# Attention with a mixture of experts: the sixth batch's late routing steps and scatters, and the fifth's last scatters, moved behind pair 28

## The chip, the cores and the metric

The kernel runs on one NeuronCore of a Trainium2 chip. Its engines work at the same time, each through its own instructions in program order: PE (TensorE, matrix products), DVE (VectorE), ACT (ScalarE), POOL (GpSimd) and SP (SyncE, which here only issues transfers). The metric is the device time of one execution in microseconds.

## The reference, cut to what matters

```python
B, H, S, D = 8, 8, 576, 64
scores = (rotate(q) @ rotate(k).T) / sqrt(D)
attn = exp(scores - max(scores)); attn = attn / sum(attn)
x = transpose(attn @ v).reshape(B * S, H * D)          # 4608 tokens of 512
logits = x @ w_gate + modality_bias[modality_id]       # 8 experts
e_idx = argmax(logits); gate_w = softmax(logits)[e_idx]
for e in range(8):                                     # each token: its one expert
    out[e_idx == e] = gate_w * (relu(x @ w1[e]) @ w2[e])
```

## The kernel before, in words

**Attention.** The 64 heads go through as 32 pairs (`n` = 0 to 31), four to a batch. For a pair, POOL rotates q and k by four passes over tiles of 128x1152 (`rope_`, lines 461 to 469; ACT makes the high part of the result between the last two), SP copies the two halves of the result across the partitions (`swap`, line 477, tile SW), PE makes nine score tiles (`scores`, line 492), DVE copies each out of PSUM with its minimum (`rowmin`, line 501, tile `sc`), ACT takes the exponentials (`expo`, line 510), PE turns them over (`fill`, line 515; F0 to F3 are four such fills), ACT and DVE each copy one of the two banks of a fill (`evac`, lines 548 and 452), PE multiplies by v (`AV`, line 573) and makes the pair's output rows and gate logits (`outp`, line 608). PSUM is four tiles of two banks, `ps0` to `ps3`, which stand in the traces as ps and in the lists of order as ps_126 to ps_129; `take` gives a step the slot that the table SLOTS names if its banks are free, and another free one if not.

**Routing of a batch.** After its fourth pair (3, 7, ..., 31) a batch is routed in fifteen small steps, RK0 to RK14 (`route`): logits, one-hot choice (RK6, three POOL operations, tile OH), ranks within the expert (RK8, seven small matmuls on PE with a PSUM bank of their own), RK9 (DVE adds the running counts and so frees the bank), RK10 (ACT), RK11 (`own_rank`, POOL), RK12 (DVE, the gate values into VAL), RK13 (DVE, tile `of`), RK14 (POOL, row numbers `oi`). Then VO writes the token numbers and gates beside the batch's rows in the DRAM tensor X (`vout`, two small transfers, lines 640 and 641), and for each of five groups of tokens BK loads the group's rows from X into one of two buffers XL (`back`, lines 756 and 758, 257 KB, the fifth half that) and SC scatters them to the rows of their experts in the DRAM tensor XS (`scatter`, line 738, an indirect transfer that only POOL issues). The buffers are given out in turn, so a BK waits until the SC before the last has read its buffer.

**The expert stage.** A first plan (`plan0`, POOL and DVE, done at about 405 us) covers five supers of 512 or 256 rows out of the first five batches alone; it needs the fifth batch's scatters, not the sixth's. The rest is planned after the eighth batch. Super 0 runs inside the last pair, super 1 is `m_plain`, the next are `m_super`. A super's results leave PSUM through ACT into the `sc` buffers (`m_store`, line 1113) and go to the output by indirect transfers that POOL issues (line 1114). The pool has NSS = 4 `sc` buffers, so the sixth result tile (super 1, fourth tile) takes the buffer of the second (super 0, second tile).

**What sets the order.** Every step of attention and routing is a job with a key, `KEYS[name]` or the pair's own entry in EDGE, plus 14.438 (PER) times the pair's number; jobs are sorted by key and written out in that order on all engines. Keys behind those of the last pair's end (about 472.56) come after the PSUM of attention is given back. The batch's last pair gives its routing keys, so the fifth batch's are pair 19's and the sixth's pair 23's; at key 404.26 pair 28 begins. In the trace a key is roughly the microsecond at which its step runs.

Of the kernel before, what the change touches and what calls it, by code (L numbers as in the profile page):

```python
# [19 lines left out]
B, H, S, D = 8, 8, 576, 64  # L20
# [110 lines left out]
        "LD1": -42.214,  # L131
    },
    19: {
    },
    23: {
    },
    25: {
        "RE": 11.575, "F2": 13.246, "A_F2": 14.351, "B_F2": 14.486, "RI": 16.427, "AVB": 18.725, "OTB": 20.519, "OUT": 26.426,
# [92 lines left out]
def tile_attention_moe(ctx: ExitStack, tc: tile.TileContext, qk, v, mod, wg, mb, w1, w2, rope, cf, ci, out):  # L231
    nc = tc.nc
# [405 lines left out]
    def vout(b, eng=nc.sync):  # L638
        xd = X[b * S:(b + 1) * S, DM:XU]
        eng.dma_start(out=xd[0:512, :].rearrange("(p j) w -> p j w", j=4), in_=VAL[:, b, 0:4, :].bitcast(F32))  # L640
        eng.dma_start(out=xd[512:576, :], in_=VAL[0:64, b, 4, :].bitcast(F32))
# [93 lines left out]
    def scatter(b, j):  # L735
        oi = bt_[b]["oi"]
        n = P if j < 4 else 64
        inst = nc.gpsimd.indirect_dma_start(  # L738
            out=XS, out_offset=bass.IndirectOffsetOnAxis(ap=oi[0:n, j:j + 1], axis=0),
            in_=xl[b, j][0:n], in_offset=None, bounds_check=E * RS - 1, oob_is_err=False).ins  # L740

        for _b, x in placed:
            tc.declare_no_dep(inst, x, reason="rows of other tokens")
        placed.append((b, inst))
        if b >= NPL:
            for x in taken:
                tc.declare_no_dep(inst, x, reason="the first plan's blocks lie before the rows of later batches")
# [4 lines left out]
    def back(b, j, eng=nc.sync):  # L752
        t = xl[b, j] = XL[len(xl) % 2]
        xd = X[b * S:(b + 1) * S, 0:XU]
        if j < 4:
            eng.dma_start(out=t[:, 0:XU], in_=xd[0:512, :].rearrange("(p j) w -> j p w", j=4)[j])
        else:
            eng.dma_start(out=t[0:64, 0:XU], in_=xd[512:576, :])

    def pads():  # L760
        nc.vector.tensor_copy(CNT, RUN[0:1, B, :])
        for e in range(E):
            r = nc.sync.value_load(CNT[0:1, e:e + 1], min_val=0, max_val=E * RS - BLK)
            inst = nc.sync.dma_start(out=XS[bass.ds(r, BLK), 0:XU], in_=ZR[:, :]).ins
            for _b, x in placed:
                tc.declare_no_dep(inst, x, reason="rows behind those of the tokens")
            for x in taken:
                tc.declare_no_dep(inst, x, reason="the first plan's blocks are full")
            placed.append((B, inst))
# [692 lines left out]
    def J(k_, nm, n, f, *a):  # L1462
        jobs.append((k_ + PER * n, len(jobs), f, a))
# [30 lines left out]
    for n in range(NPAIR):  # L1494
        def K_(nm, f, *a):
            J(EDGE.get(n, {}).get(nm, KEYS[nm]), nm, n, f, *a)

        for u in range(9):
            K_(f"S{u}", scores, n, u)
            K_(f"MN{u}", rowmin, n, u)  # L1500
            K_(f"EX{u}", expo, n, u)
        for f in ("F0", "F1", "F2", "F3", "FA", "FB"):
            K_(f, fill, n, f)
            for g in range(2):
                K_(f"{'AB'[g]}_{f}", evac, n, f, g)
        for w in range(2):
            c = "AB"[w]
            K_(f"AV{c}", AV, n, w)
            K_(f"OT{c}", avout, n, w)
            K_(f"EV{c}", ev, n, 1 - w)  # L1510
        K_("OUT", outp, n)
        for w in range(2):
            K_("R" + "EI"[w], rsum, n, w)
        if n > 0:
            for part, nm in ((1, "T1"), (0, "T2"), (2, "R"), (3, "HI"), (4, "LO")):
                K_(nm, rope_, n, part)
            for i in range(2):
                K_("SW" + "HL"[i], swap, n, i)
        K_("LV", loadv, n)
        if n > 2:  # L1520
            K_("LD1", load, n, 1)
            K_("LD", load, n, 0)
        if n % 4 == 3:
            K_("BIAS", bias, n // 4)
            K_("XO", xout, n // 4)
            steps = [(f,) for f in route(n // 4)]
            scats = [(scatter, n // 4, j) for j in range(5)]
            if n == z:

                planned = plan()  # L1530
                steps[0:2] = [(each, lambda f: f(), *steps[0:2])]
                late = steps + [(lambda: [vout(B - 1, nc.gpsimd)] + [(back(B - 1, j, nc.gpsimd), scatter(B - 1, j)) for j in range(5)] + [pads()],)] + [(each, next) + ((planned, None),) * 4] * 13
                continue
            for i, x in enumerate(steps):
                K_(f"RK{i}", *x)
            eng = nc.sync if n // 4 < B - 2 else nc.gpsimd
            K_("VO", vout, n // 4, eng)
            for i, x in enumerate(scats):
                K_(f"BK{i}", back, n // 4, i, eng)
                K_(f"SC{i}", *x)  # L1540
# [209 lines left out]
```

## Time and profile before

| | us |
|---|---|
| median of three runs (lowest, highest) | 882.19 (881.38, 886.98) |
| the profiled execution, its own time | 884.29 |
| its span in the trace | 882.5 |

A row of the trace gives the start in microseconds from the span's start, the duration, the engine, the line of the kernel, the operation, its output and inputs, and in brackets how long the engine stood idle before it and what ended that. PE is the engine with the most work; a microsecond in which it stands idle is one that the kernel could lose.

### The profile page before, as it was taken

The page shows a single profiled execution, that of the slowest core. Times are in us where ns is not written, and L with a number is a line of the kernel's source. Part 1 is how long each engine was busy: PE and PEld are TensorE (multiplying, and loading weights), DVE is VectorE, ACT ScalarE, POOL GpSimd, SP SyncE. Part 2 cuts the span into 40 slices and gives each one's busy share as a digit, 9 for nine tenths or more (in the row PEclk, how much of TensorE's full clock was granted, in tenths as well). Part 3 has the DMA queues.
Part 4 walks back from the last instruction along what each step waited for, and adds up shares of the span by engine and source line. Part 5 has one row for each costly group of instructions (what it writes and reads, how often), then busy time and mean ns, then how long its engine had stood idle before and what let it go on. Part 6 is the DMA issues. An engine that isn't in the chain of part 4 may idle for free.

```text
span 882.5 us, 24889 instructions
## 1 busy us (share of the span) xinstructions
PE 833.9 (94%) x9528; PEld 688.7 (78%) x9528; DVE 708.9 (80%) x1595; ACT 612.2 (69%) x1311; POOL 453.5 (51%) x365
## 2 busy tenths in 40 slices
PE   2899999999999999888999999999999999999992
PEld 2677777777777777676778989898989898989882
DVE  6888898888898888777888577989898998979360
ACT  2898989889888888777975446464656474748360
POOL 2999979989899898999511211024201112020100
PEclk9999999999999999999999999999999999999996
DMA  8877868979788797875877961377955413530520
GB/s 262 229 231 193 260 169 259 265 211 283 205 262 245 215 279 205 249 213 171 251 213 187 328 181 49 60 219 224 282 139 186 114 38 88 169 101 8 186 73 14
DMA packets 116330, 165.80 MB, mean 188 GB/s; under 512 B 31180, under 2 KB 76894, under 8 KB 116204
## 3 DMA queue, kind: packets, MB, share of 16 engines
q1 hardware_dynamic: 107468, 139.18, 55.2%
q0 software_dynamic: 7392, 23.34, 7.5%
q8 instruction: 77, 1.26, 0.6%
q10 hardware_dynamic: 1344, 1.62, 0.6%
q14 instruction: 49, 0.40, 0.1%
HBM read 118.14 MB, written 34.70 MB: 173 GB/s over the span
## 4 chain that ended last, share of the span: by engine, by line
PE 79%; DMA 5%; POOL 4%; ACT 4%; DVE 3%; issue 2%; SPq 1%; ACTq 0%; POOLq 0%; DVEq 0%
PE psY L1326 20%; PE ps L573 15%; PE psH L1202 14%; PE ps L492 13%; PE ps L515 9%; PE ps L608 2%; DMA SW<-HL 2%; PE psY L1202 2%; ACT P L510 1%; PE psH L1084 1%; PE psY L1103 1%; DMA ST<-in_rope_dram 1%; POOL HL L469 1%; DVE sc L501 1%; DMA ST<-in_moe_w_dram 1%
## 5 line engine op out<-in xcount | busy, mean ns | idle before, releaser
L501 DVE CUSTOM_DVE_ANT_1 sc<-ps,ZERO 128x576 f32<-128x576 f32 x288 | 206.6, 748 | 24.0 <-PE ps L492 11.3
L510 ACT ACTIVATE P<-sc,mn 128x576 f32<-128x576 f32 x256 | 195.5, 767 | 5.9 <-DVE mn L501 4.7
L492 PE MATMUL ps<-HL 64*128 64x288 f32 x960 | 167.9, 309 | 13.7 <-ACT HL L452 10.8
L492 PE MATMUL ps<-SW 64*128 64x288 f32 x960 | 168.1, 309 | 7.6 <-DMA SW<-HL 7.5
L1114 POOL DMA_INDIRECT out_dram<-sc,ix x36 | 43.4, 1206 | 222.1 <-ACT sc L1113 215.4
L492 PEld LDWEIGHTS ps<-HL 64*128 64x128 f32 x960 | 134.4, 188 | 19.5 <-ACT HL L452 10.8
L492 PEld LDWEIGHTS ps<-SW 64*128 64x128 f32 x960 | 134.3, 188 | 11.9 <-issue 9.4
L573 PE MATMUL ps<-PH,AT 128*64 128x320 f32 (+1 forms) x1024 | 139.6, 415 | 4.0 <-DVE PH L548 3.7
L1202 PE MATMUL psH<-HL,W1H 128*128 128x256 f32 x600 | 126.4, 279 | 0.4 <-ACT HL L452 0.4
L1202 PE MATMUL psH<-HL,W1L 128*128 128x256 f32 x400 | 111.6, 279 | 0.0
L573 PEld LDWEIGHTS ps<-PH,AT 128*64 128x64 f32 x1024 | 68.4, 137 | 53.1 <-DVE PH L548 7.0
L548 DVE COPY PH<-ps 128x512 f32<-128x512 f32 (+1 forms) x160 | 98.3, 630 | 11.0 <-PE ps L515 8.8
L452 ACT ACTIVATE PH<-ps 128x512 f32<-128x512 f32 (+1 forms) x160 | 85.3, 551 | 29.6 <-PE ps L515 26.0
L515 PEld LDWEIGHTS ps<-idf,P 64*128 64x128 f32 x2304 | 86.0, 138 | 20.7 <-ACT P L510 8.5
L1326 PE MATMUL psY<-W2L,SW 128*128 128x512 f32 x256 | 101.3, 396 | 0.0
L1326 PE MATMUL psY<-W2H,SW 128*128 128x512 f32 x256 | 100.9, 394 | 0.0
L515 PE MATMUL ps<-idf,P 64*128 64x64 f32 x2304 | 97.3, 225 | 2.8 <-ACT AT L452 1.7
L1202 PEld LDWEIGHTS psH<-HL,W1H 128*128 128x128 f32 x600 | 98.8, 188 | 1.1 <-ACT HL L452 0.6
L469 POOL TENSOR_TENSOR HL<-ST,HL 128x1152 fp32r<-128x1152 f32 x31 | 82.5, 2660 | 24.4 <-ACT HL L452 24.3
L465 POOL TENSOR_TENSOR ST<-ST 128x1152 f32<-128x1152 f32 x30 | 79.5, 2651 | 1.1
L738 POOL DMA_INDIRECT XS<-XL,oi x40 | 44.8, 1120 | 66.1 <-DMA XL<-X 45.2
L1202 PEld LDWEIGHTS psH<-HL,W1L 128*128 128x128 f32 x400 | 75.2, 188 | 0.0
(286 smaller groups left out, 1829.6 us busy)
## 6 DMA issues: line engine op xcount, KB each, us to landing
ST<-in_moe_w_dram SPq DMA_DIRECT2D x88, 512.0 KB
ST<-in_qk_dram SPq DMA_DIRECT2D x62, 576.0 KB
SW<-HL SPq DMA_DIRECT2D x124, 216.0 KB
AT<-in_v_dram SPq DMA_DIRECT2D x32, 256.0 KB
X<-X SPq DMA_DIRECT2D x8, 1024.0 KB
XL<-X SPq DMA_DIRECT2D x24, 257.0 KB
XG<-XS SPq DMA_DIRECT2D x40, 128.0 KB
XS<-ZR SPq DMA_DIRECT2D x8, 514.0 KB
```

The source lines that it names most:

```text
L452: return nc.scalar.activation(o, i, AF.Copy, scale=scale)
L465: e.tensor_tensor(a, a, b, op=ALU.add)
L469: e.tensor_tensor(d["HL"][:, 1, o], a, d["HL"][:, 0, o].bitcast(F32), op=ALU.subtract)
L492: nc.tensor.matmul(ps[:, g, 0:288], t[:, wq, q0:q0 + P], t[:, wk, k0:k0 + 288], start=(m == 0), stop=(m == len(L) - 1))
L501: nc.vector.tensor_tensor_reduce(sc, d.pop(("S", u))[:, :, 0:288], ZERO.unsqueeze(2).to_broadcast([P, 2, 288]), 1.0, FMAX, ALU.add, ALU.mi ...
L510: nc.scalar.activation(p, sc.rearrange("p a b -> p (a b)"), AF.Exp, bias=mn, scale=-1.0, accum_out=d["sum"][:, u:u + 1])
L515: nc.tensor.transpose(ps[:, g, c:c + 64], src[r, k0:k0 + P], idf[r, r])
L548: alone(d["at", f], g, (nc.vector.tensor_copy if g else acopy)(o, i).ins, int(f[1] in "23B"))
L573: i = nc.tensor.matmul(pa[hh * 64:hh * 64 + 64, 0:c1 - c0], d["V"][:, hh, kt, :], r, start=(kt == 0), stop=(kt == 4))
L738: inst = nc.gpsimd.indirect_dma_start(out=XS, out_offset=bass.IndirectOffsetOnAxis(ap=oi[0:n, j:j + 1], axis=0), in_=xl[b, j][0:n], in_off ...
L1202: nc.tensor.matmul(ps[b][:, r * BLK:r * BLK + BLK], w[:, c, f0:f0 + P], x[:, c, :], start=(first and r == 0 and c == 0 and i == 0), stop=( ...
L1326: nc.tensor.matmul(po[t], hx[:, c, o:o + P], w[:, c, :], start=(k == 0 and c == 2 * q and i == 0), stop=(k == 3 and c == 2 * q + 1 and i = ...
```

## The change

The fifth batch (index 4, pair 19) keeps its steps, but its loads and scatters take another order, 0, 1, 3, 2, 4, and the last two scatters come 9 and 31 key units later. The sixth batch (index 5, pair 23) has RK6 to RK8 some three units earlier (RK9 two later), RK10 to RK14 22 to 64 units later, and VO, the loads and the scatters after them, in the order 3, 4, 2, 1, 0, at keys 461 to 470, just ahead of the seventh batch's. Its VO and its five BK are issued by POOL in place of SP.

```diff
     19: {
+        "BK0": 71.4, "BK1": 71.5, "BK3": 95.0, "BK2": 116.0, "BK4": 131.0,
+        "SC3": 113.825, "SC2": 128.215, "SC4": 152.075,
     },
     23: {
+        "VO": 129.3, "BK3": 130.0, "BK4": 130.1, "BK2": 132.5, "BK1": 133.0, "BK0": 137.0,
+        "RK6": 45.016, "RK7": 49.391, "RK8": 52.824, "RK9": 58.16, "RK10": 79.988, "RK11": 109.721, "RK12": 128.347, "RK13": 128.956,
+        "RK14": 129.684, "SC3": 130.859, "SC4": 132.359, "SC2": 132.942, "SC1": 136.961, "SC0": 137.506,
     },
...
-            eng = nc.sync if n // 4 < B - 2 else nc.gpsimd
+            eng = nc.sync if n // 4 < B - 3 else nc.gpsimd
             K_("VO", vout, n // 4, eng)
             for i, x in enumerate(scats):
                 K_(f"BK{i}", back, n // 4, i, eng)
```

The new lines move the line numbers behind them by five (line 701 is 706 in the lists of the change). Three places show what moves.

On PE, in pair 27, before: the six score matmuls into ps_126 and the fill of ps_129 (F3), then the sixth batch's ranks (tile OH) in ps_127:

```order
L492 MATMUL ps_126<-HL_87 128x288
L492 MATMUL ps_126<-SW_89 128x288
L492 MATMUL ps_126<-HL_87 128x288
L492 MATMUL ps_126<-SW_89 128x288
L492 MATMUL ps_126<-HL_87 128x288
L492 MATMUL ps_126<-SW_89 128x288
L515 MATMUL ps_129<-idf,P_120 128x64 x16
L701 LDWEIGHTS UT
L701 MATMUL ps_127<-OH,UT 128x48
L703 LDWEIGHTS ON
L703 MATMUL ps_127<-OH,ON 128x40
```

And now, the end of the ranks and what follows it:

```order
L708 LDWEIGHTS ON
L708 MATMUL ps_127<-OH,ON 128x16
L708 LDWEIGHTS ON
L708 MATMUL ps_127<-OH,ON 128x8
L497 MATMUL ps_126<-HL_87 128x288
L497 MATMUL ps_126<-SW_89 128x288
L497 MATMUL ps_126<-HL_87 128x288
L497 MATMUL ps_126<-SW_89 128x288
L497 MATMUL ps_126<-HL_87 128x288
L497 MATMUL ps_126<-SW_89 128x288
L520 MATMUL ps_129<-idf,P_120 128x64 x16
L613 MATMUL ps_128<-RW,AT 64x72 x18
```

The ranks moved ahead of six matmuls and a fill, and the pair's output matmuls (line 613, before 608) now follow the fill at once. At their new place bank 1 of ps_127, which DVE empties, is not free yet in the order of the jobs, so `take` gives them bank 0, which ACT empties.

On POOL, at the same time, before (tiles ST and HL are the rotation; `rk` is RK11, `pes` the first plan):

```order
L463 TENSOR_TENSOR ST_75<-ST_75 128x1152
L738 DMA XS<-XL_82,oi 39424x528
L687 TENSOR_TENSOR vv<-vv,vm 128x40
L688 TENSOR_SCALAR OH<-vv 128x32
L689 TENSOR_SCALAR OH<-vv 64x8
L469 TENSOR_TENSOR HL_86<-ST_74,HL_86 128x1152
L461 TENSOR_TENSOR ST_75<-ST_75,ST_74 128x1152
L465 TENSOR_TENSOR ST_75<-ST_75 128x1152
L738 DMA XS<-XL_83,oi 39424x528
L718 TENSOR_TENSOR rk<-rk,OH 128x40
L738 DMA XS<-XL_82,oi 39424x528
L831 TENSOR_SCALAR pes<-pes 1x1
```

And now:

```order
L692 TENSOR_TENSOR vv<-vv,vm 128x40
L693 TENSOR_SCALAR OH<-vv 128x32
L694 TENSOR_SCALAR OH<-vv 64x8
L468 TENSOR_TENSOR ST_75<-ST_75 128x1152
L474 TENSOR_TENSOR HL_86<-ST_74,HL_86 128x1152
L743 DMA XS<-XL_82,oi 39424x528
L466 TENSOR_TENSOR ST_75<-ST_75,ST_74 128x1152
L470 TENSOR_TENSOR ST_75<-ST_75 128x1152
L836 TENSOR_SCALAR pes<-pes 1x1
```

Two of the fifth batch's scatters and RK11 are gone from this stretch; the scatters come back behind the plan, and the one-hot choice is ahead of a rotation pass. From here to the last rotation pass POOL issues three scatters in place of five, and none in place of three between there and the sixth batch's new tail.

On POOL, behind the last rotation, the sixth batch's whole tail now stands ahead of the seventh's. It begins with:

```order
L645 DMA X<-VAL 512x1x2
L646 DMA X<-VAL 64x2
L723 TENSOR_TENSOR rk<-rk,OH 128x40
L733 CAST oi<-of 128x5
L761 DMA XL_83<-X 128x514
L763 DMA XL_82<-X 64x514
L743 DMA XS<-XL_83,oi 39424x528
L743 DMA XS<-XL_82,oi 39424x528
L761 DMA XL_83<-X 128x514
L743 DMA XS<-XL_83,oi 39424x528
L761 DMA XL_82<-X 128x514
L743 DMA XS<-XL_82,oi 39424x528
```

It goes on with the load and the scatter of group 0, the seventh batch's VO, its cast, two loads, super 0's first store to the output (line 1119, before 1114), the seventh batch's other loads and scatters, and then the second store. Before, the seventh batch's VO stood first in this row, and the stretch held its ten transfers only. On SP the sixth batch's two VO and five BK transfers are gone.

## Rows read from the trace of the kernel before

**Rows 1.** Page, part 1: busy us of each engine (share of span) xinstructions
```profile
PE 833.9 (94%) x9528; PEld 688.7 (78%) x9528; DVE 708.9 (80%) x1595; ACT 612.2 (69%) x1311; POOL 453.5 (51%) x365
```

**Rows 2.** Busy time in one stretch: engines' busy us, TensorE clock, DMA share, GB/s
```profile
380.00:450.00 70.00, 62.84 (x1004) 47.52 (x1002) 53.54 (x160) 55.93 (x146) 49.45 (x60) 1.00 0.71 208
```

**Rows 3.** Timeline of PE: start, us, engine line op out<-in [idle before <-releaser]
```profile
387.12 0.40 PE L492 MATMUL ps<-HL 64*128 64x288 f32 x1 [0.87 <-ACT AT L452]
...
389.36 0.20 PE L701 MATMUL ps<-OH,UT 128*128 128x48 bf16 x1 [1.08 <-DVE PH L548]
...
389.60 0.86 PE L608 MATMUL ps<-RW,AT 64*64 64x72 f32 x36
...
391.44 1.95 PE L573 MATMUL ps<-PH,AT 128*64 128x256 f32 x16 [0.34 <-DVE RUN L710]
...
416.53 1.64 PE L515 MATMUL ps<-idf,P 64*128 64x64 f32 x46 [1.68 <-ACT AT L452]
...
443.06 0.37 PE L492 MATMUL ps<-SW 64*128 64x288 f32 x1 [1.54 <-DMA SW<-HL]
```

**Rows 4.** Timeline of ACT, 374 to 446 us
```profile
385.96 0.85 ACT L452 ACTIVATE PH<-ps 128x512 f32<-128x512 f32 x2
...
414.99 1.16 ACT L452 ACTIVATE HL<-ST 128x1152 fp32r<-128x1152 f32 x1 [4.01 <-POOL ST L465]
```

**Rows 5.** Timeline of DVE, 374 to 500 us
```profile
397.66 0.18 DVE L721 RECIPROCAL VAL<-ee 128x5 f32<-128x5 f32 x1
397.76 0.14 DVE L783 TENSOR_REDUCE pes<-cmp 1x5 f32<-1x40 f32 x1
...
460.64 0.70 DVE L1063 STREAM_TRANSPOSE XG<-XG 128x512 f32<-128x512 f32 x1
```

**Rows 6.** Timeline of POOL, 385 to 480 us
```profile
397.99 0.18 POOL L831 TENSOR_SCALAR pes<-pes 1x1 f32<-1x1 f32 x1 [1.48 <-DVE pes L783]
...
410.71 0.18 POOL L728 CAST oi<-of 128x5 int32<-128x5 f32 x1
411.18 1.10 POOL L738 DMA_INDIRECT XS<-XL,oi  x1 [0.29 <-POOL oi L728]
412.31 2.64 POOL L465 TENSOR_TENSOR ST<-ST 128x1152 f32<-128x1152 f32 x1
```

**Rows 7.** Timeline of SP's queue, 380 to 505 us
```profile
435.14 0.54 SPq L756 DMA_DIRECT2D XL<-X  x1
435.77 4.55 SPq L477 DMA_DIRECT2D SW<-HL  x4
```

**Rows 8.** DMA issues by line: count, KB each, median us from issue to landing
```profile
XL<-X POOLq DMA_DIRECT2D x8, 257.0 KB, 5.5
...
XS<-XL,oi POOLq DMA_INDIRECT x40, 6.3
out_dram<-sc,ix POOLq DMA_INDIRECT x36, 4.6
```

**Rows 9.** Timeline of POOL, 465 to 640 us
```profile
481.09 1.15 POOL L756 DMA_DIRECT2D XL<-X  x2 [0.44 <-issue]
...
501.26 0.59 POOL L756 DMA_DIRECT2D XL<-X  x1 [6.54 <-DMA XS<-XL,oi]
...
513.78 0.98 POOL L1114 DMA_INDIRECT out_dram<-sc,ix  x1 [0.30 <-issue]
...
593.92 1.03 POOL L738 DMA_INDIRECT XS<-XL,oi  x1 [8.19 <-DMA XL<-X]
```

**Rows 10.** Timeline of ACT, 495 to 552 us
```profile
535.73 0.69 ACT L1113 ACTIVATE sc<-psY,ix 128x512 f32<-128x512 f32 x1 [0.70 <-issue]
537.13 0.60 ACT L452 ACTIVATE AT<-psH 128x512 f32<-128x512 f32 x1 [0.71 <-PE psH L1202]
538.53 0.60 ACT L452 ACTIVATE AT<-psH 128x512 f32<-128x512 f32 x1 [0.80 <-PE psH L1202]
...
541.26 1.06 ACT L452 ACTIVATE W1H<-ST 128x1024 fp32r<-128x1024 f32 x1 [0.67 <-ACT HL L452]
```

## The prediction

> **What bounds the kernel now.** I read the page's busy times first: PE works 94% of the span [rows 1], so a change of this kind can only move PE's idle time, or make more of it. Then the stretch that the change touches, by windows: from 380 to 450 us PE is busy 62.84 of 70 us and idle 7.2 [rows 2]. The timeline of PE shows where those go, and the reader is to see the releaser in the brackets [rows 3]: 0.87 us for an ACT copy, 1.08 ahead of the sixth batch's ranks, 0.34 for the step that frees the ranks' bank, 1.68 behind an ACT copy at 416.53, 1.54 for the swapped tile SW at 443.06; the other 1.7 us of the 7.2 are waits that no edited step releases. The 1.68 is really POOL's: ACT stood 4.01 us at 414.99 for the rotation pass of line 465, and the copy that PE wanted was queued behind it [rows 4]. So in this stretch PE is bound, with POOL's rotations and SP's swaps coming last now and then.
>
> **The ranks go ahead of a fill (gain 1.4 us).** Before, the ranks wanted the bank that DVE empties, and DVE came to it late: PE waited 1.08 us, and the matmuls behind the ranks, the pair's output and the product with v, could not pass [rows 3]. Now the ranks stand before the six score matmuls. Those had to wait 0.87 us anyway for ACT to empty ps_126, until 387.12 [rows 3]; the ranks' new bank is emptied by ACT in the copy at 385.96, the first of two in 0.85 us, so by about 386.5 [rows 4], and OH is earlier than before, as POOL makes it ahead of a 2.64 us pass. The ranks (some 0.25 us, 389.36 to 389.60) thus fit into the 0.87 us, and the 1.08 us has nothing left that it waits for: the output matmuls only want a tile whose minimum DVE took before. The 0.34 us goes too, since the product with v takes another slot than that of the ranks. Together 1.42. Bounds: 1.42 above; below nothing, if the output or the product is then held by DVE's copies, which keep their order and are what PE waited for.
>
> **POOL is lighter, but little of it counts (gain 0.5 us).** Ahead of the plan two scatters of about 1.1 us and RK11 are gone. That buys nothing: POOL already waited 1.48 us at 397.99 for DVE's `pes` [rows 6], so leaving earlier it waits longer. What counts is that `pes` itself comes earlier with PE (the 1.4 us of above) and without the VAL reciprocal ahead of it (0.18 us, of which 0.1 until the next starts [rows 5]). Behind the plan POOL runs without a gap to the pass at 412.31 that ACT waited for [rows 6]. In that piece one scatter (1.10) stays, a group of the fifth batch in place of one of the sixth, and the `oi` cast with the wait behind it goes (0.18 + 0.29 = 0.47). So this pass ends 1.4 + 0.1 + 0.5 = 2.0 us earlier, PE comes there 1.4 earlier, and of its 1.68 us wait 0.5 to 0.6 falls away. Bounds: 0 to 0.6.
>
> **SP is lighter (gain 0.6 us).** The 4.55 us of swaps for the last pair stood behind a BK of the sixth batch that took 0.63 us of SP, from 435.14 to 435.77 [rows 7]; PE then waited 1.54 for them at 443.06 [rows 3]. Without it they start 0.63 earlier. The five loads and VO leave SP's other swaps unhindered as well, but PE waited for none of those. Less traffic (the sixth batch's loads and scatters, four and a half groups of 257 KB [rows 8] each way, 2.3 MB, out of a stretch where DMA is busy 0.71 [rows 2]) may add something; bounds 0 and the whole 1.54.
>
> **DVE pays at the other end (loss 0.35 us).** RK12 and RK13, 0.18 us each by the VAL row [rows 5], move to the transpose of super 0's rows at 460.64, where DVE works without a gap until super 0's weights are split. Behind them stand the weight splits that PE's first expert matmuls want. I take the full 0.35; nothing at the least.
>
> **The tail on POOL (cost 0, up to 10 us).** The sixth batch's seven loads and writes and five scatters now stand ahead of the seventh's on POOL, and what is queued behind both is super 0's second store, at 513.78 before [rows 9]. Who waits for it: its `sc` buffer is the one that ACT needs for super 1's fourth tile, at 535.73, and ACT has 0.71 + 0.80 + 0.67 = 2.2 us of idle time from there until the copy at 541.26 [rows 10]. So the store may land until 535.7 + 2.2 = 537.9 without cost; beyond that ACT, PE's next, is late by the rest.
>
> When does it land? VAL now comes just ahead of the transposes at 460.64 [rows 5], so the tail starts at 461. Of it POOL must wait, in turn, for VO's landing, for one scatter (group 3, whose buffer the third load takes) and for four loads. The landings are 6.3 and 5.5 us at the median [rows 8]: 6.3 + 4 x 5.5 = 28.3; VO's I put at half a load's, 3; the issues between are two of 0.6 and four scatters of 1.1 [rows 6, 9], 5.6. That is 37 us, so the seventh batch's VO comes at 498, and its first loads, 4.2 later, at 502 in place of 481.09 [rows 9]: 21 us late. From those loads to the second store it was 513.78 - 481.09 = 32.7 us, which puts the store at 534.9 and its landing, 4.6 on [rows 8], at 539.5. In that stretch two scatters took 7.5 us each (6.54 of wait and 1.0 of issue [rows 9]); they now lie behind 515 us, when the transfers of the weights thin out, and at the median of 6.3 take 2.4 less: 537.1. That is 0.8 us inside the limit, so I take 0. Both ends: the seventh batch's loads can be absorbed further (nothing), or the sixth's four loads take 8.2 us each, as the one of the eighth batch did that POOL waited for at 593.92 [rows 9]: 10.8 later, landing at 548, cost 10. The gains of above move both times alike.
>
> For a transfer that POOL issues the Trainium skill (DMA: Bandwidth & Descriptors, section Anatomy of one DMA — SWDGE (gpsimd) path) gives about 2.0 us and the bytes at 436 GB/s, 2.6 us for 257 KB. The rows show twice that, 5.5 and 6.3, on a loaded chip [rows 8], so I go by the rows. By the page the five waits would be an estimated 13 us in place of 28.3, the store would land some 15 us inside the limit, and the cost and the rival that rests on it would be gone.
>
> The fifth batch's late scatters cost nothing: the last is at key 426.4 and the first plan's table is read from 434.05 (13.525 ahead of key 447.58, where pair 31 begins), 7.6 later, where a scatter lands in 6.3 [rows 8]; if it took 8 us, SP would stand about 0.4 longer. The eighth batch's tail waits for its own gate values long behind all this.
>
> **The sum.** 1.4 + 0.5 + 0.6 - 0.35 = 2.15 us less than the profiled execution's 884.29, so 882.1; that execution stands 2.1 us above the median of the runs shown, 882.19, and against the median it is 880.0.
>
> **The rivals.**
> 1. *The tail on POOL comes too late.* One mechanism: super 0's second store lands behind 537.9 us, ACT holds super 1's fourth tile for its buffer, and the copies that PE's next products need are queued behind it. For it speaks that the middle estimate is 0.8 us inside the limit and that loads of 8.2 us occur; against it that DMA is emptier from 520 us on. At the full 10 us it gives 880.0 + 10 = 890; in the middle, 5 us, 885. It decides the sign from a landing at 540.1, 2.2 us behind the limit.
> 2. *The gains are taken up by the next wait.* PE then stands at the output or the product with v for DVE, at 416 for ACT's own copies, and at 443 for swaps that the traffic, not SP, holds. For it: DVE is busy 53.5 and ACT 55.9 of the 70 us [rows 2], and each gain hides behind another engine's queue. It gives 880.0 + 2.15 = 882.2.
> 3. *The traffic matters more than I say.* 2.3 MB leaves a loaded stretch, and the swap that PE waited 1.54 us for lands in time, with 0.9 us more to be had there; 2.3 MB enters the stretch in which super 0's and 1's weights are loaded. It gives 879 at the good end, and about 884 if a weight load is late by 4 us, a scatter's worth less a little.
>
> **How the numbers follow.** My forecast 0.5 (878 to 881.5, its own range by the terms' bounds), rival 1 0.27, rival 2 0.17, rival 3 0.06. The low end, 877, is all terms at their upper bounds (1.42 + 0.6 + 1.54 = 3.6) and a run that lies 1.5 us low, as runs of one kernel do; the high end, 886, leaves out the later half of rival 1. About 0.15 lies outside. One per cent, 8.8 us, is about what a measurement of this kernel can tell from no change. Faster by it would need 873.4, beyond all terms: 0.02. Slower by it needs 891, rival 1 at its end: 0.04. The rest, 0.94, is the same.
>
> **What the profile of the changed kernel would show.** The ranks on PE right behind the scores of ps_128 with no wait over 0.3 us, and no idle time of 1 us ahead of the output matmuls: else the first term is wrong. POOL's wait at `pes` longer than 1.48 us, and ACT's wait for line 465 (470 there) ending 2 us earlier. The last pair's swaps issued 0.6 us earlier against PE, and PE's wait there under 1 us. On POOL super 0's second store near 530 us; if ACT stands idle ahead of super 1's fourth result tile for a store on POOL, rival 1 is at work, and its price is that wait less 2.2 us. The forecast is wrong if PE's idle time between 380 and 450 us is not about 2 us smaller, or if it grows between 530 and 560.

## The result, and the profile after

The changed kernel takes 872.32 us (median of 6 runs, 869.25 to 874.26), the kernel before 881.98 beside it (6 runs). The ratio is 0.9871, with a 95% interval of 0.9832 to 0.9909: faster by 1.3%. That is below the range of the forecast, 877 to 886. The profiled execution of the changed kernel took 872.7 us with a span of 870.9.

The page's first part and the window that stood in [rows 2], for the changed kernel (its lines are 5 higher than before's; columns of the window: length, then busy time with instruction counts of PE, PEld, DVE, ACT, POOL, then the granted clock, DMA share, GB/s):

```profile
span 870.9 us, 24881 instructions
PE 834.2 (96%) x9528; PEld 689.6 (79%) x9528; DVE 708.8 (81%) x1595; ACT 611.5 (70%) x1311; POOL 460.5 (53%) x372
...
380.00:450.00 70.00, 67.63 (x1044) 51.73 (x1042) 56.15 (x164) 58.29 (x151) 45.22 (x56) 0.98 0.66 197
```

PE is busy for as long as before, 834.2 against 833.9 us [rows 1], so what was saved is idle time: 36.7 us of the span in place of 48.6. In the window PE stands idle 2.4 us in place of 7.2 [rows 2]; the nine profiles in which this stretch is unchanged (last table) have 4.2 to 7.2 there, 5.8 in the mean.

Timeline of PE, the rows that answer to [rows 3]: the ranks, the output product behind them, the wait for ACT that is left, and the output product of the next pair but two; no row from 438 to 446 us has a wait, so the 1.54 us for the swap is gone.

```profile
386.00 0.20 PE L706 MATMUL ps<-OH,UT 128*128 128x48 bf16 x1
387.50 0.86 PE L613 MATMUL ps<-RW,AT 64*64 64x72 f32 x36
...
413.19 2.28 PE L520 MATMUL ps<-idf,P 64*128 64x64 f32 x48 [1.60 <-ACT AT L457]
...
442.27 0.86 PE L613 MATMUL ps<-RW,AT 64*64 64x72 f32 x36
```

POOL, ACT and SP there, in three timelines, against [rows 4], [rows 6] and [rows 7]: POOL's wait at `pes` is 0.83 us (1.48 before), ACT waits for POOL's line 470 until 411.65 (414.99), and SP issues the last pair's four swaps at 431.72 with no BK ahead of them (435.77).

```profile
394.82 0.18 POOL L836 TENSOR_SCALAR pes<-pes 1x1 f32<-1x1 f32 x1 [0.83 <-DVE pes L788]
```
```profile
411.65 1.16 ACT L457 ACTIVATE HL<-ST 128x1152 fp32r<-128x1152 f32 x1 [3.30 <-POOL ST L470]
```
```profile
431.72 2.59 SPq L482 DMA_DIRECT2D SW<-HL  x4
```

Then the tail on POOL. Its timeline, 455 to 560 us: the sixth batch's VO, the seventh's VO, super 0's first store and its second, which stood at 513.78 before [rows 9].

```profile
457.64 0.84 POOL L645 DMA_DIRECT2D X<-VAL  x1 [13.82 <-DVE VAL L726]
...
497.62 0.80 POOL L645 DMA_DIRECT2D X<-VAL  x1
...
505.12 1.04 POOL L1119 DMA_INDIRECT out_dram<-sc,ix  x1 [0.30 <-issue]
...
531.65 0.98 POOL L1119 DMA_INDIRECT out_dram<-sc,ix  x1 [0.30 <-issue]
```

And who waits for that second store, by the timelines of ACT and PE: ACT stands 3.35 us ahead of super 1's fourth tile (0.70 before, [rows 10]), and PE 2.08 us at the eighth batch's ranks, where it stood 0.49 before. The changed kernel's two rows, and then before's row of the ranks:

```profile
534.50 0.69 ACT L1118 ACTIVATE sc<-psY,ix 128x512 f32<-128x512 f32 x1 [3.35 <-DMA out_dram<-sc,ix]
```
```profile
547.90 0.18 PE L706 MATMUL psY<-OH,UT 128*128 128x48 bf16 x1 [2.08 <-DVE OH L694]
```
```profile
550.18 0.18 PE L701 MATMUL psY<-OH,UT 128*128 128x48 bf16 x1 [0.49 <-DVE OH L689]
```

All of this together is small: from 550 us to the last product the changed kernel is 2.3 us ahead of the profile of before. The larger part lies behind the last store. Of the kernel before, POOL's last row in its timeline, and then the lines that close the program (1647 is the branch behind the last super, 1746 the program's end), by source line (count, shortest/median/longest in ns, first and last start):

```profile
867.14 0.98 POOL L1427 DMA_INDIRECT out_dram<-sc,ho  x1 [0.44 <-issue]
```
```profile
L1647 POOLq EVENT_SEMAPHORE  x4: 17/43/2677, 868.2 to 871.1; - x4
...
L1647 POOLq INC_SWDGE_SEM  x1: 2200/2200/2200, 871.2 to 871.2; - x1
```
```profile
L1746 POOLq DRAIN  x3: 46/109/8241, 873.4 to 882.2; - x3
```

The same of the changed kernel:

```profile
864.84 0.98 POOL L1432 DMA_INDIRECT out_dram<-sc,ho  x1 [0.43 <-issue]
```
```profile
L1652 POOLq EVENT_SEMAPHORE  x4: 17/43/2118, 865.9 to 868.3; - x4
...
L1652 POOLq INC_SWDGE_SEM  x1: 480/480/480, 868.3 to 868.3; - x1
```
```profile
L1751 POOLq DRAIN  x3: 46/109/1217, 868.9 to 870.6; - x3
```

From the end of the last store to the end of the span it is 882.5 - 868.1 = 14.4 us before and 870.9 - 865.8 = 5.1 us now. Nothing computes there. POOL waits on a semaphore, by its place for the landing of that store, then comes INC_SWDGE_SEM, 2200 ns and now 480, then the long DRAIN, 8241 ns and now 1217, and the other engines end behind POOL. These 9.3 us are four fifths of the 11.6 by which the two spans differ, and no step that the diff moves stands there.

### The profile page after: what moved, and what is told of

It reads as the page before. It is cut to its first block, busy times and chain, and to the rows that moved or that the text cites. A ratio compares the mean times of both kernels' runs of the same rounds, so it can differ in the third digit from the quotient of the medians.

```text
span 870.9 us, 24881 instructions
## 1 busy us (share of the span) xinstructions
PE 834.2 (96%) x9528; PEld 689.6 (79%) x9528; DVE 708.8 (81%) x1595; ACT 611.5 (70%) x1311; POOL 460.5 (53%) x372
## 4 chain that ended last, share of the span: by engine, by line
PE 71%; POOL 11%; issue 5%; DMA 5%; DVE 4%; ACT 2%; SPq 1%; POOLq 0%; DVEq 0%; ACTq 0%
PE psY L1331 21%; PE psH L1207 14%; PE ps L578 12%; PE ps L497 10%; PE ps L520 7%; POOL HL L474 3%; POOL ST L468 2%; PE psY L1207 2%; POOL ST L470 2%; POOL ST L466 2%; PE ps L613 2%; DMA SW<-HL 2%; PE psH L1089 1%; PE psY L1108 1%; DMA AT<-XS 1%
## 5 line engine op out<-in xcount | busy, mean ns | idle before, releaser
L1119 POOL DMA_INDIRECT out_dram<-sc,ix x36 | 43.8, 1217 | 200.2 <-ACT sc L1118 192.9
L743 POOL DMA_INDIRECT XS<-XL,oi x40 | 46.6, 1165 | 76.3 <-DMA XL<-X 55.7
```

Source lines behind the costliest of these rows:

```text
L743: inst = nc.gpsimd.indirect_dma_start(out=XS, out_offset=bass.IndirectOffsetOnAxis(ap=oi[0:n, j:j + 1], axis=0), in_=xl[b, j][0:n], in_off ...
```

## The experiments

Three theories for the end. A: what POOL has issued as transfers sets it (the change gives POOL seven more, 107 in place of 100 in the profile's part on DMA issues). B: where POOL's code comes to lie. C: chance of the run. The stages have their own questions: whether the tail's transfers had to go to POOL, what the ranks' move alone is worth, and whether the late store is what ACT pays for.

**1. The transfers back on SP, the steps moved as in the change.**

```diff
-            eng = nc.sync if n // 4 < B - 3 else nc.gpsimd
+            eng = nc.sync if n // 4 < B - 2 else nc.gpsimd
```

> The changed kernel with the sixth batch's VO and BK transfers given back to SP (all moved steps stay where the change puts them). Every theory: the middle of the program gains as in the changed kernel up to the second store of super 0, and ACT's 3.35 us wait for that store's buffer is gone, because nothing of the sixth batch stands ahead of it on POOL; so the last product comes 3 to 4 us earlier than before (changed kernel: 2.3). On the end of the program, from POOL's last store to the end of the span (14.4 us after its end before, 5.1 changed): theory A, the number of transfers that POOL issues sets it: 14 us again, time about 878.5. Theory B, the place of POOL's code sets it: POOL has as few instructions as before, 14 us, 878.5. Theory C, it is the weather of a run: either.

891.31 us, ratio 1.008 (1.0046 to 1.0113), and the end is long again: INC_SWDGE_SEM 2196 ns, DRAIN 8241. A and B said so, and C allowed it, so all three are left. All three were wrong on the time, since they had the stages gain as in the changed kernel. What they said of the late store held: from 541 to 550 us PE needs 9.21 us, as before. Waits of SP's queue from 440 to 480 us, and PE's timeline:

```profile
SPq L761 <- DMA XS<-XL,oi: 7.0, 1, 7.0
SPq L645 <- DVE of L729: 4.1, 1, 4.1
```
```profile
491.97 0.58 PE L1207 MATMUL psH<-HL,W1H 128*128 128x256 f32 x1 [6.68 <-ACT HL L457]
```

From 390 to 445 us it does as well as the changed kernel (52.69 us; the changed kernel's lengths are in the last table). Then SP, which also loads the experts' weights, stands behind the sixth batch's `of` and behind scatters that must free the XL buffers; the weights come late, PE waits 6.68 us ahead of the first expert product, and from the output product at 445 us to 541 it needs 106.7 us in place of 95.7. So in this kernel the steps can be moved this late only because POOL takes the transfers; the edit that looked like a detail carries the change.

**2. Seven more transfers by POOL in the kernel before, and nothing else.** They copy rows of X into a scratch tensor that nobody reads, behind super 5's stores.

```diff
+    SCR = dram.tile([7 * P, XU], F32, name="SCR")
...
         for t in range(4):
             m_store(s, t, po[t])
+        if s == 5:
+            for i in range(7):
+                nc.gpsimd.dma_start(out=SCR[i * P:i * P + P, :], in_=X[i * P:i * P + P, 0:XU])
```

> The kernel before with seven more transfers that POOL issues (128 rows of X into a scratch buffer each), behind the stores of super 5; nothing else is changed. Theory A (the count of POOL's transfers sets the end): the end shrinks from 14.4 to about 5 us, time about 873 although nothing of the change is in it. Theory B (place of POOL's code): short too. Theory C: either, not tied to this edit. If the end stays at 14 us the count alone is not it, and the time is 882 to 884.

874.83 us, ratio 0.9896 (0.9858 to 0.9934): most of the change's gain without the change. By source line, the end:

```profile
L1651 POOLq INC_SWDGE_SEM  x1: 436/436/436, 872.7 to 872.7; - x1
```
```profile
L1750 POOLq DRAIN  x3: 46/109/1054, 873.1 to 874.7; - x3
```

**3. Seven memsets by POOL at the same place, and 4. the kernel before once more.**

```diff
+    SCR = cst.tile([1, 8], F32, name="SCR")
...
+        if s == 5:
+            for i in range(7):
+                nc.gpsimd.memset(SCR, float(i))
```

> The kernel before with seven one-row memsets on POOL (into a scratch tile of 8 numbers), behind the stores of super 5: seven more instructions on POOL, no more transfers. Theory A: the end stays at 14 us and the time at 882. Theory B (place of POOL's code): the end shrinks to about 5 us, 873. Theory C: either.

> The kernel before, unchanged, once more beside itself. Theories A and B: the end takes 14 us after POOL's last store again, ratio 1.000 within 0.3 per cent. Theory C (the end's length is chance): in some of the executions it is some 9 us shorter, so the times fall into two groups near 873 and 882.

882.70 us, ratio 0.9991 (0.9968 to 1.0013), and 883.56 us, 1.0006 (0.9982 to 1.0029). In both the DRAIN takes 8241 ns and INC_SWDGE_SEM 2196. B falls, since seven more instructions do nothing (and experiment 8 below, with as many instructions on POOL as experiment 2, has a long end). C falls, since none of the 33 executions of the kernel before here came near 873: they took 879.4 to 888.5 us.

**5 to 8. How many transfers, or how large.** The range of experiment 2 becomes 1, 3 and 14 (with a scratch tensor of fourteen blocks for the 14; the first pair of lines below, for 1), and once it stays 7 with a single row in each (the second pair).

```diff
-            for i in range(7):
+            for i in range(1):
...
-                nc.gpsimd.dma_start(out=SCR[i * P:i * P + P, :], in_=X[i * P:i * P + P, 0:XU])
+                nc.gpsimd.dma_start(out=SCR[i * P:i * P + 1, :], in_=X[i * P:i * P + 1, 0:XU])
```

> The kernel before with one more transfer that POOL issues (128 rows of X into a scratch buffer), behind the stores of super 5. The seven of the earlier run cut POOL's closing DRAIN from 8241 to 1054 ns and its INC_SWDGE_SEM from 2196 to 436. Theory A1, the closing time falls in proportion to what is added: DRAIN 8241 - 7187 / 7 = 7210 ns, time about 881.5. Theory A2, it has two lengths and changes over somewhere between 0 and 7 added: 8241 or about 1100.

> The same with three more transfers. Theory A1 (in proportion): DRAIN 8241 - 3 x 1027 = 5160 ns, time about 879. Theory A2 (two lengths): 8241 or about 1100.

> The same with fourteen more transfers. Theory A1 in its plain form would give less than nothing, so either the floor of about 1050 ns, or, if the count runs round (theory A1 with a period), a DRAIN that has started anew near 8 us. Theory A2: about 1100 ns, time 873 to 875.

> The kernel before with seven more transfers by POOL at the same place, each of a single row of X (2 KB) in place of 128. If the number of transfers counts: DRAIN about 1054 ns as with the seven whole ones, time 873 to 875. If the descriptors or packets in them count: hardly less than 8241, time 882.

Single executions: 881.27, 873.66, 875.04 and 882.76 us, beside 884.85 for the kernel before. The two ends at the change-over, one and three added, and the one with seven single rows:

```profile
L1750 POOLq DRAIN  x3: 46/109/8322, 870.3 to 879.2; - x3
```
```profile
L1750 POOLq DRAIN  x3: 46/109/727, 870.2 to 871.5; - x3
```
```profile
L1750 POOLq DRAIN  x3: 46/109/8812, 870.9 to 880.3; - x3
```

Neither form of A foresaw all of this, though A2 had the change-over, and of experiment 8's two cases the second came. The DRAIN grows by 81 ns with one more transfer and by 571 = 7 x 81.6 with seven small ones; with three large ones it falls to 727, and then grows again by 81.7 each: 1054 with seven, 1626 with fourteen. Before's 8241 is 73 + 100 x 81.7, and 100 is the number of POOL's transfers in the whole program. INC_SWDGE_SEM follows the same count, 196 + 20 each: 2196 with 100, 2336 with 107, 356 where the DRAIN says 8. So POOL closes a program as if it went through a list of its transfers, 0.1 us for each that is still on it; and at some point a list that has become too long is cleared on the way.

Where that happens shows in POOL's timeline. The store that is issued then comes late: with three transfers added it is the very last one, 2.76 us of idle time in place of 0.44.

```profile
862.98 0.98 POOL L1431 DMA_INDIRECT out_dram<-sc,ho  x1 [10.78 <-ACT sc L1430]
866.72 0.99 POOL L1431 DMA_INDIRECT out_dram<-sc,ho  x1 [2.76 <-ACTq L1651]
```

In the changed kernel it is the second store of the last super but two, 1.85 us in place of 0.38, the seventh transfer from the end (the first line below is before's):

```profile
828.71 0.98 POOL L1114 DMA_INDIRECT out_dram<-sc,ix  x1 [0.38 <-ACT sc L1113]
```
```profile
825.00 1.02 POOL L1119 DMA_INDIRECT out_dram<-sc,ix  x1 [26.29 <-ACT sc L1118]
827.88 0.99 POOL L1119 DMA_INDIRECT out_dram<-sc,ix  x1 [1.85 <-ACT sc L1118]
829.16 0.98 POOL L1119 DMA_INDIRECT out_dram<-sc,ix  x1 [0.30 <-ACT sc L1118]
```

**9. and 10. The changed kernel again, and one transfer of 896 rows.** What fills the list, transfers or rows? The rows added ahead of the stalled store point to rows (table below); one transfer with as many rows as seven tells it apart.

```diff
+    SCR = dram.tile([7 * P, XU], F32, name="SCR")
...
+        if s == 5:
+            nc.gpsimd.dma_start(out=SCR, in_=X[0:7 * P, 0:XU])
```

> The changed kernel once more, beside the three below. Time about 872.5, ratio to before about 0.988 (0.987 measured); POOL's closing DRAIN 1217 ns and INC_SWDGE_SEM 480 ns again, since the transfers are the same. ACT's wait for the buffer of super 0's second store 3 to 4 us again.

> The kernel before with one more transfer by POOL behind the stores of super 5, of 896 rows of X, as many rows as the seven of the earlier run carried. Theory R (POOL keeps a list of its transfers, with room for a sum of rows between 256 and 384 above that of before, and clears it when the room is used up; the closing DRAIN takes 73 ns and 81.7 for each transfer still listed, INC_SWDGE_SEM 196 and 20): room is used up at the same store as with seven, twelve transfers stay listed, DRAIN 1054 ns, INC_SWDGE_SEM 436 ns, time 873 to 875, ratio 0.990. Theory N (the number of transfers uses the room up, 103 do): 101 transfers, DRAIN 8322 ns, time 882, ratio 1.000. The stages are those of before in both, so the ratio of the changed kernel to this one is what the change brings outside the end: 1.3 us by the profiles (0.15 per cent).

870.12 us, ratio 0.9862 (0.9832 to 0.9892), and 874.35 us, 0.9910 (0.9878 to 0.9942), beside the same runs of before. Experiment 9 has the same end as the changed kernel's first profile, but its ACT waited longer for the late store, 4.24 us where 3 to 4 were expected:

```profile
533.48 0.69 ACT L1118 ACTIVATE sc<-psY,ix 128x512 f32<-128x512 f32 x1 [4.24 <-DMA out_dram<-sc,ix]
```

The end of experiment 10:

```profile
L1650 POOLq INC_SWDGE_SEM  x1: 436/436/436, 865.9 to 865.9; - x1
```
```profile
L1749 POOLq DRAIN  x3: 46/109/1054, 866.3 to 867.9; - x3
```

To the nanosecond what rows foretold (1054, 436) and not what their number did (8322). All kernels together; "rows added" is against before's program, "of these ahead of the stalled store" takes off the rows of 128 in each store from that one to the end; "on the list" is (DRAIN - 73) / 81.7:

| kernel | POOL transfers | rows added | ahead of the stalled store | DRAIN, ns | INC_SWDGE_SEM, ns | on the list |
|---|---|---|---|---|---|---|
| before, 1, 3, 4, 12 | 100 | 0 | no stall | 8241 | 2196 to 2200 | 100 |
| 5: one | 101 | 128 | no stall | 8322 | 2216 | 101 |
| 8: seven single rows | 107 | 7 | no stall | 8812 | 2336 | 107 |
| 6: three | 103 | 384 | 384 - 1 x 128 = 256 | 727 | 356 | 8 |
| 2: seven | 107 | 896 | 896 - 5 x 128 = 256 | 1054 | 436 | 12 |
| 7: fourteen | 114 | 1792 | 1792 - 12 x 128 = 256 | 1626 | 576 | 19 |
| 10: one of 896 rows | 101 | 896 | 896 - 5 x 128 = 256 | 1054 | 436 | 12 |
| the changed kernel, 9, 11 | 107 | 4 x 128 + 64 + 576 = 1152 | 1152 - 7 x 128 = 256 | 1217 | 476 to 480 | 14 |

In the five kernels with a stall it comes at the first store for which more than 256 rows beyond before's are asked. Before's program ends 256 to 383 rows short of a cleared list. The size of a row does not matter: of the changed kernel's 1152 rows the 576 that VO writes have 8 bytes, the others 2 KB, and its stall agrees with those of the other four kernels only if a row of 8 bytes weighs 0.78 to 1.22 of one of 2 KB.

**11. The second store earlier.** In the changed kernel super 0's second tile is now written out behind the first scatter of the seventh batch. On POOL its store moves ahead of seven transfers; on PE, DVE and ACT the order of the instructions stays.

```diff
     J(end + 0.1, "moe", z, m_l2, 0, 0)
+    J(end + 5.0, "moe", z, m_l2, 0, 1)
...
-    m_l2(0, 1)
```

> The changed kernel with super 0's second store issued behind the first scatter of the seventh batch instead of behind its last, about 511 us instead of 531.65. Its buffer is then free long before ACT wants it for super 1's fourth tile. If POOL's late store is what cost 1.6 us at the eighth batch's ranks (rival 1): ACT's 3.35 us wait and DVE's 5.55 are gone, the marks of PE from 541 to 550 us lose nothing, time about 871, ratio to before 0.986. If something else held ACT there, 872.5.

869.33 us, ratio 0.9842 (0.9812 to 0.9872), the fastest of all, though the times alone do not part it from the changed kernel beside it (0.9862). The trace does: the store is at 513.42 on POOL, ACT's wait is 0.71 us again, and PE needs 9.20 us from 541 to 550, as before, where the changed kernel needed 10.79 and 10.80 in its two profiles.

```profile
513.42 0.98 POOL L1119 DMA_INDIRECT out_dram<-sc,ix  x1 [0.30 <-ACT W1H L457]
```
```profile
534.13 0.69 ACT L1118 ACTIVATE sc<-psY,ix 128x512 f32<-128x512 f32 x1 [0.71 <-PE psY L1331]
```

**12. The ranks alone.**

```diff
     23: {
+        "RK6": 45.016, "RK7": 49.391, "RK8": 52.824, "RK9": 58.16,
     },
```

> The kernel before with only the sixth batch's RK6 to RK9 moved to the keys of the change (the ranks' matmuls ahead of a probability fill); VO, BK and SC stay, on SP. First term of the forecast alone: from the outputs at 370 us to those at 389.6 PE needs 1.4 us less than before (1.0 to 1.5 less than the mean of the unchanged runs), and nothing more is gained from there to 445. POOL's end as before: DRAIN 8241 ns. Time about 880.5.

882.70 us, a single execution; DRAIN 8241. From the output product at 370 us to the next one PE needs 17.30 us, to the hundredth what the changed kernel needs; the ranks again stand without a wait:

```profile
386.44 0.20 PE L702 MATMUL ps<-OH,UT 128*128 128x48 bf16 x1
387.94 0.86 PE L609 MATMUL ps<-RW,AT 64*64 64x72 f32 x36
```

From there to 445 us it needs 56.96, 1.3 more than the mean of the unchanged stages, and over both stages together 74.26, inside their range of 73.43 to 75.57. In this one profile, in which the granted clock also fell (0.89 from 405 to 420 us), the gain did not last.

## Why the prediction was wrong, step by step

Experiments 2 to 8 and 10 leave the stages untouched, so with before's own profile there are nine profiles of them (their spread shows what one profile can tell). Lengths in us between the starts of PE rows: the output products at 370.40, 389.60 and 445.40 of before's profile, the first expert products at 489.50, 541.13 and 550.33, and the last product's second half:

| stage | before's profile | nine unchanged, mean (range) | changed, its two profiles | 11 | forecast | found |
|---|---|---|---|---|---|---|
| 370 to 390, the ranks | 19.20 | 18.85 (18.77 to 19.20) | 17.30, 17.31 | 17.29 | -1.4 | -1.55 |
| 390 to 445, POOL and SP lighter | 55.80 | 55.71 (54.63 to 56.78) | 54.77, 52.84 | 52.50 | -0.5 - 0.6 | -1.9 |
| 445 to 490, RK12, RK13 on DVE | 44.10 | 43.78 (43.66 to 44.10) | 43.75, 43.75 | 43.75 | +0.35 | 0.0 |
| 490 to 541 | 51.63 | 51.54 (50.40 to 51.99) | 51.24, 52.26 | 51.79 | 0 | +0.2 |
| 541 to 550, the tail's store | 9.20 | 9.20 (9.20 to 9.21) | 10.79, 10.80 | 9.20 | 0 | +1.6 |
| last store's end to the span's end | 14.4 | 14.4 to 15.2 (list not cleared), 4.1 to 6.4 (cleared) | 5.1, 5.7 | 5.5 | no term | -8.7 or more |

**The step that failed is the sum itself: it had no term for the program's end.** The forecast read the trace only as far as PE's waits, from 380 to 600 us, and took the 14.4 us behind the last store as fixed. They lie in the longest stretch in which PE stands idle. The change gave POOL seven transfers of 1152 rows together, by the table of experiments enough for its list to be cleared ahead of the end. By that table, 86 fewer on the list at 101.7 ns each are 8.7 us; the rest of the 9.3 is the landing of the last store, 2677 against 2118 ns, which differs from run to run.

**Outside the end the sum was near by luck, since its errors offset each other.** It said -2.15; the five stages give -1.55 - 1.9 + 0.2 + 1.6 = -1.65.

- *The ranks, -1.4.* Right in mechanism and size: experiment 12 shows 1.55 less than the unchanged mean with that edit alone (17.30 against 18.85), just past the upper bound of 1.42, and the waits are gone.
- *POOL and SP lighter, -1.1.* Right in mechanism, too small: -1.9, near the upper bounds of 0.6 and 1.54. ACT's copy behind POOL's line 470 came 3.3 us earlier where 2 were expected (2.1 of it is there at the output product ahead, 389.60 to 387.50), and the wait for the swap went entirely. One sign came the other way: POOL's wait at `pes` was to grow beyond 1.48 us and shrank to 0.83, as DVE's `pes` came 3.2 us earlier (397.76 to 394.56) where 1.5 were expected. The two profiles differ by 1.9 here. Both have PE's 1.6 us wait for ACT near 412 us, but behind it the granted clock fell in the first, to 0.50 (the 1.2 GHz level) from 414 to 417 us, and not in the second. Between the output products around it PE needs 12.72 us in the first (405.79 to 418.51) and 11.25 in the second (404.80 to 416.05), 1.5 of the 1.9. Windows of the changed kernel and of experiment 9:

```profile
405.00:420.00 15.00, 13.40 (x236) 11.05 (x236) 10.43 (x30) 10.44 (x26) 14.70 (x7) 0.89 0.56 179
```
```profile
405.00:420.00 15.00, 13.39 (x250) 10.23 (x246) 12.08 (x37) 11.36 (x31) 14.82 (x7) 1.00 0.59 172
```

- *DVE at the other end, +0.35.* Wrong: nothing was lost (43.75 us in all but one of the unchanged profiles within 0.1, and in the changed ones).
- *The tail on POOL, 0.* Wrong: +1.6, and rival 1 happened. The chain itself was forecast well: the seventh batch's VO at 498 (497.62), its loads at 502 (503.69), the store at some 532.5 (531.65). What failed is "the gains of above move both times alike". The chain began 3.4 us earlier than the forecast's 461, but it is paced by landings and took 40.0 us to the seventh VO in place of 37; ACT's need followed PE and came 3.9 us earlier, at 531.86 in place of 535.73. ACT's idle time there, taken as 2.2 us, covered only 1.1: the wait is 3.35, 0.70 is usual, 1.59 came through. In experiment 9 ACT waited 4.24 and the same 1.60 came through, so 1.9 was covered; why the price did not follow the wait stays open. That the late store is the cause is shown by experiment 11, in which nothing else moved.
- *By the page of the Trainium skill that the forecast weighed* (DMA: Bandwidth & Descriptors, section Anatomy of one DMA — SWDGE (gpsimd) path: about 2.0 us and the bytes at 436 GB/s) the store would have landed 15 us inside the limit; it landed behind it. The seven single rows of experiment 8 landed in 2.0 us, as the page's fixed part says (DMA issues, the last number):

```profile
SCR<-X POOLq DMA_DIRECT2D x7, 2.0 KB, 2.0
```

  With the DMA engines 0.96 busy (474 to 497 us) POOL waited 4.9 to 6.1 us for each of the sixth batch's later loads.

**The forecast's own signs of being wrong** both came: PE's idle time between 380 and 450 us shrank by 4.8 us in place of 2 (by 3.3 against the mean of the nine), and it grew between 530 and 560, by the wait ahead of 548 us. **Rival 2** may hold of the ranks alone (experiment 12, one profile, so not shown) and does not hold of the whole: over the first two stages the three profiles of the moved steps with POOL's transfers need 69.8 to 72.1 us, the nine unchanged ones 73.4 to 75.6. **Rival 3** can't be told apart: the DMA share of the window fell from 0.71 to 0.66 (0.69 in experiment 9), but what that brought lies in the same stage as the lighter queues. **The chances** gave 0.02 to faster by over 1%, since no term could reach it; without the end's 8.7 of the 9.7 us the change would by this estimate have been the same within 1% (experiments 9 and 10, whose ends are both short, stand at 0.9862 and 0.9910, with intervals that overlap).

## What to carry to other kernels

Look at what stands behind the last store before adding up stages: here 14.4 of 882 us, on an engine that had nothing to do. When a change moves transfers from one queue to another, count them and their rows for the whole program, since a cost at the program's end can hang on both. And a chain of transfers in which each waits for the landing of another does not move up with the engines it serves: it gains less, and uses up the slack of whoever waits for its last link.

## What the runs showed of the hardware

- POOL's closing work goes by the transfers it has issued: INC_SWDGE_SEM 196 ns and 20 for each, DRAIN 73 ns and 81.7 for each, over 8 to 107 on the list. By this a hundred transfers cost 10.2 us at the end of the program. The list itself is inferred from these counts; no row shows it.
- The list was cleared in all five kernels whose transfers had more than a certain sum of rows (256 to 383 above that of this program), and in no other; POOL then stood 1.3 to 2.3 us longer than usual at one issue, and eight transfers, that one among them, stayed listed. Off the critical path that is cheap: a single transfer of 896 rows that nobody reads brought the kernel before to 0.9910 (0.9878 to 0.9942). The Trainium skill (DMA: Bandwidth & Descriptors, section SWDGE vs HWDGE vs iDMA) says that GpSimd appends the descriptors of its transfers to rings in SBUF; a room that is counted in rows fits that, but no run here shows the rings themselves. Bytes are not what is counted, since rows of 8 bytes weighed as much as rows of 2 KB.
- The clearing can hit the path: with three transfers added it fell on the last store, and 2.3 of the 10 us came back as its delay.
